# Token order, output stores and PSUM buffers of a fused pooled-attention and expert-routing kernel

## The chip, the core and the metric

The kernel runs on one core of a Trainium2 chip. The core has five engines that work side by side, each in the order of its own instruction list: TensorE for matmuls (PE; its weight loads are shown as PEld), VectorE (DVE), ScalarE (ACT), GpSimd (POOL) and SyncE (SP). They meet through semaphores. Sixteen DMA engines move data between HBM and SBUF; POOL and SP issue the transfers. Matmuls write to PSUM, which has 8 banks of 512 fp32 numbers in each of 128 partitions, and DVE and ACT read it out. The metric is device time in microseconds (us) of one execution.

## What is computed

```python
# q, k, v: (8, 8, 576, 64) float32: batch, head, token, dim
k_p = k.reshape(B, H, 72, 8, D).mean(axis=3)      # 576 tokens pooled to 72
v_p = v.reshape(B, H, 72, 8, D).mean(axis=3)
attn = softmax(q @ k_p^T / 8)                      # (B, H, 576, 72)
x = (attn @ v_p).transpose(0, 2, 1, 3).reshape(4608, 512)
# routing: normalised x against 8 normalised expert embeddings, / tau
expert_idx = argmax(logits, axis=1); gate_w = softmax(logits)[expert_idx]
for e in range(8):                                 # w1 (8,512,1024), w2 (8,1024,512)
    out[idx == e] = gate_w * (relu(x[idx == e] @ w1[e]) @ w2[e])
```

## The kernel before

The work goes in eight batches of 576 tokens. A batch has two halves: attention with routing, and the expert network (`ffn`). For each batch the kernel guesses one expert for all tokens from the mean of pooled v (steps GM, GC, GL, GD), and loads only that expert's weights. A loop at the end would add other experts' tokens; with these inputs it has no iterations.

**Loads.** POOL issues them in a fixed order: V0, K0, Q0, V1, and then for each batch b a group: PK (read the guessed expert number into a register), W1 of b, K of b+1, Q of b+1, W2 of b, V of b+2. They convert fp32 in HBM to fp16 in SBUF. So group b can't go before the guess of batch b, which needs V of b, which was the last load of group b-2. There are three buffers each for W1 and W2, two each for V, K and Q.

**Attention of one batch.** DVE adds V and K in groups of eight tokens (steps VA, VB, KA, KB, lines L301 to L315) and transposes q in 32x32 blocks (QT, L385). PE computes scores in four steps SC (two halves of 288 tokens, two groups of four heads, L415), each of which writes two double PSUM tiles. ACT takes the exponential (EX, L428), two per SC. For each of five chunks of 128 tokens (the fifth has 64 new ones), PE multiplies by pooled v (PV, L443) into a double tile, DVE normalises (XM, L451 and L453), PE transposes the result back (XT, L461), DVE copies it to SBUF (XE, L466) and ACT squares it for the norms (SQ, L472). PE's RT (L490, L495) gives the routing logits, and the steps RE, NA, NB, NC, ND make the gate `gm_all`.

**Token order.** Token s = 18*p + t of a batch (p of 32, t of 18) stands at column 32*t + p after QT, and all later steps keep that order. A chunk of 128 columns is therefore four values of t times 32 values of p: its 128 rows of `out` lie 18 rows apart in four interleaved sets.

**The expert network of one batch.** Eight steps H on PE (L548: 8 matmuls of 288 columns each, both halves into one double tile), each followed by a ReLU over 576 columns on ACT or DVE (HE, L557 or L559). Four steps Y (L563, 8 matmuls of 512 columns), two of them sharing one double tile, each followed by scaling with the gate (YE, L575 or L577) and a store of 128x512 fp32 by SP (ST, L622). The last 64 tokens go as YL (L569), which puts the two halves of the 512 output columns on partitions 0 to 63 and 64 to 127. DVE scales the first half (YF, L577), ACT the second (YG, L575), and SP stores both (SL, L644). The tokens' gates lie on partitions 64 to 127, so SP copies them to partitions 0 to 63 with a DMA of 64 x 4 bytes (NE, L539, `gl_all`); YF waits for it.

**PSUM.** One ring of four double tiles `pa` of 2 banks each serves every step.

**What sets the order.** `Plan.order` places every step by planned busy times (the numbers in `add`), priorities and free buffers, and the instructions of each engine are then written out in that order. On the chip each engine runs its list strictly in that order.

Of the kernel before, what the change touches and what calls it, by code (L numbers as in the profile page):

```python
# [142 lines left out]
def kernel(  # L143
# [36 lines left out]
    psum = Ring(lambda i: ps.tile([128, 1024], FP32, name=f"pa{i}"), 4)  # L180
# [91 lines left out]
    def attention(b, base):  # L272
# [52 lines left out]
        if b == 0:  # L325
            pv_, pk_ = Buf(psum), Buf(psum)
# [11 lines left out]
        else:  # L338
            add(n("VA"), 'DVE', 1.14, pr(-0.5), lambda: halve(vr.tile, 4), [n("V")], uses=[vr],
                late=0.1)  # L340
            add(n("VB"), 'DVE', 0.95, pr(-0.5), v_fold, [n("VA")], takes=[vp], uses=[vr],
# [3 lines left out]
            add(n("KB"), 'DVE', 1.0, pr(-0.2), k_fold, [n("KA")], takes=[kp], uses=[kr],  # L345
# [3 lines left out]
        pg = Buf(psum)  # L349
# [27 lines left out]
        add(n("GD"), 'DVE', 0.35, pr(-0.5), choose, [n("GL")], uses=[pg], late=0.1)  # L377
        add(n("GE"), 'DVE', 0.2, pr(0.5), onehot, [n("GD")], late=0.1)
# [12 lines left out]
        pk = Buf(psum)  # L391
# [10 lines left out]
        add(n("KE"), 'DVE', 0.25, pr(0.0), lambda: nc.vector.tensor_copy(  # L402
# [5 lines left out]
        for half in range(2):  # L408
            for a in range(NQ):
                pair = [Buf(psum), Buf(psum)]  # L410

                def score(a=a, half=half, pair=pair):
                    for c in range(2):
                        for m in range(QG):
                            nc.tensor.matmul(  # L415
                                out=pair[m // 2].tile[0:G, m % 2 * 512:m % 2 * 512 + HALF],
                                lhsT=kpT.tile[ts(m, R), a, c, :],
                                rhs=qT.tile[ts(m, R), a, ts(half, T // 2), c, :],
                                start=(c == 0), stop=(c == 1))

                f = 0.02 + 0.2 * half + 0.1 * a
                add(n("SC", half, a), 'PE', 0.35, pr(f), score,
                    [n("KE"), n("QT", a, half)], takes=pair, uses=[qT, kpT], late=0.22,
                    mode='r32')
                for i in range(2):
# [3 lines left out]
                            out=t.tile[:, :, ts(half, HALF)],  # L429
                            in_=p.tile[0:G].rearrange("g (r c) -> g r c", r=2)[:, :, 0:HALF],  # L430
# [5 lines left out]
        for c in range(NC):  # L436
            px, r, x, pt = Buf(psum), Buf(r_r), Buf(x_r), Buf(psum)
# [49 lines left out]
        pl = Buf(psum)  # L487
# [36 lines left out]
        def gate():  # L524
# [5 lines left out]
            nc.vector.tensor_reduce(out=gm_all[:, b], in_=lg, axis=AX.X, op=ALU.add)  # L530
            nc.vector.tensor_tensor(out=gm_all[:, b], in0=gm_all[:, b], in1=gate_all[:, b],
# [280 lines left out]
```

## Time and profile before

| what | value |
|---|---|
| median of 3 runs (lowest to highest) | 284.74 us (284.48 to 286.25) |
| the profiled execution | 285.62 us |
| its span, first to last instruction | 284.0 us |
| mean granted clock of PE | 0.879 |
| busy: PE, DVE, ACT, POOL | 205.8, 144.5, 119.4, 43.9 us |
| HBM read, written | 61.88 MB, 9.44 MB |

The span is the time that the engines' records cover. A row such as "x512 | 80.2, 313 | 33.4" gives a count, the busy time in us, the mean duration of one in ns, and the engine's idle time ahead of them. "[6.17 <-DVE y L577]" means that the engine stood idle for 6.17 us until that instruction released it. PE's clock has two levels here, 1.0 (2.4 GHz) and 0.5 (1.2 GHz). A "DMA share" is the mean busy share of the 16 DMA engines; two queues may be in one engine at the same time, so it can pass 1.

### The profile page before, as it was taken

The page shows a single profiled execution, that of the slowest core. Times are in us where ns is not written, and L with a number is a line of the kernel's source. Part 1 is how long each engine was busy: PE and PEld are TensorE (multiplying, and loading weights), DVE is VectorE, ACT ScalarE, POOL GpSimd, SP SyncE. Part 2 cuts the span into 40 slices and gives each one's busy share as a digit, 9 for nine tenths or more (in the row PEclk, how much of TensorE's full clock was granted, in tenths as well). Part 3 has the DMA queues.
Part 4 walks back from the last instruction along what each step waited for, and adds up shares of the span by engine and source line. Part 5 has one row for each costly group of instructions (what it writes and reads, how often), then busy time and mean ns, then how long its engine had stood idle before and what let it go on. Part 6 is the DMA issues. An engine that isn't in the chain of part 4 may idle for free.

```text
span 284.0 us, 5224 instructions
## 1 busy us (share of the span) xinstructions
PE 205.8 (72%) x2006; PEld 128.9 (45%) x2007; DVE 144.5 (51%) x398; ACT 119.4 (42%) x239; POOL 43.9 (15%) x59
## 2 busy tenths in 40 slices
PE   2898798868995597938995698904997069899600
PEld 1566664544563353624563354602555036476300
DVE  2178677945791557724792458514495043550200
ACT  2046285374457153453447254620542056454400
POOL 7052400700160005100060004100021000010000
PEclk9999999997999599896999599975899658999955
DMA  5979999999999937995299937992149421121120
GB/s 70 196 122 202 206 208 208 222 227 227 194 184 230 180 76 140 222 216 115 67 173 221 187 79 139 212 203 81 60 82 217 96 88 48 38 82 51 47 103 21
DMA packets 29147, 40.76 MB, mean 144 GB/s; under 512 B 4536, under 2 KB 14776, under 8 KB 29120
## 3 DMA queue, kind: packets, MB, share of 16 engines
q0 software_dynamic: 23184, 30.95, 62.5%
q1 hardware_dynamic: 5936, 9.46, 10.0%
q8 instruction: 16, 0.26, 0.4%
q14 instruction: 11, 0.09, 0.1%
HBM read 61.88 MB, written 9.44 MB: 251 GB/s over the span
## 4 chain that ended last, share of the span: by engine, by line
DMA 64%; PE 21%; DVE 4%; issue 3%; POOL 1%; ACT 1%; POOLq 1%; DVEq 0%
DMA vr<-in_v_dram 27%; DMA kr<-in_k_dram 19%; DMA gl_all<-gm_all 18%; PE pa L548 11%; PE pa L563 6%; PE pa L415 2%; DVE y L577 2%; PE pa L569 1%; POOL w L256 1%; DVE vr L301 1%; PE pa L322 1%; DVE xt_all L466 0%; ACT hT L557 0%; DVE kr L301 0%; POOLq L267 0%
## 5 line engine op out<-in xcount | busy, mean ns | idle before, releaser
L548 PE MATMUL pa<-xt_all,w 128*128 128x288 f16 x512 | 80.2, 313 | 33.4 <-DVE y L577 31.2
L548 PEld LDWEIGHTS <-w 128*128 128x128 f16 x512 | 51.3, 105 | 56.8 <-issue 41.6
L563 PE MATMUL pa<-w,hT 128*128 128x512 f16 x256 | 60.8, 383 | 4.9 <-DVE y L577 2.4
L428 ACT ACTIVATE at<-pa 72x576 f16<-72x576 f32 x64 | 37.4, 641 | 35.2 <-PE pa L415 35.1
L557 ACT ACTIVATE hT<-pa 128x576 f16<-128x576 f32 x49 | 31.8, 650 | 37.0 <-PE pa L548 35.0
L563 PEld LDWEIGHTS <-hT 128*128 128x128 f16 x256 | 24.6, 98 | 30.9 <-issue 7.3
L575 ACT ACTIVATE y<-pa,gm_all 128x512 f32<-128x512 f32 (+1 forms) x32 | 20.0, 630 | 39.9 <-PE pa L563 25.5
L472 ACT ACTIVATE sq<-x 128x512 f16<-128x512 f16 x40 | 25.1, 628 | 22.8 <-DVE x L453 18.8
L256 POOL DMA_DIRECT2D w<-in_moe_w_dram x8 | 6.4, 804 | 152.9 <-PE pa L563 120.2
L301 DVE TENSOR_TENSOR vr<-vr 72x2048 f16<-72x2048 f16 (+1 forms) x14 | 13.4, 954 | 32.8 <-DMA vr<-in_v_dram 32.6
L453 DVE TENSOR_TENSOR x<-pa,r 128x512 f16<-128x512 f32 x40 | 27.7, 691 | 1.7
L415 PE MATMUL pa<-qT,kpT 32*72 32x288 f16 x256 | 16.5, 341 | 11.4 <-DVE ssq_all L520 11.2
L385 DVE STREAM_TRANSPOSE qT<-qq 128x576 f16<-128x576 f16 x32 | 23.3, 756 | 1.5 <-DMA qq<-in_q_dram 1.5
L559 DVE TENSOR_SCALAR hT<-pa 128x576 f16<-128x576 f32 x15 | 11.4, 757 | 24.7 <-PE pa L548 24.4
L516 POOL TENSOR_TENSOR ssq_all<-ssq_all,half_c 128x5 f32<-128x5 f32 x8 | 9.9, 1242 | 51.1 <-ACT sq L472 51.1
L577 DVE TENSOR_SCALAR y<-pa,gl_all 64x256 f32<-64x256 f32 x8 | 3.8, 473 | 27.4 <-DMA gl_all<-gm_all 14.3
L466 DVE COPY xt_all<-pa 128x512 f16<-128x512 f16 (+1 forms) x40 | 14.8, 383 | 2.5 <-PE pa L461 2.4
L461 PE MATMUL pa<-ident_h,x 128*128 128x128 f16 x160 | 14.4, 224 | 2.2 <-DVE x L453 2.0
L301 DVE TENSOR_TENSOR kr<-kr 72x2048 f16<-72x2048 f16 (+1 forms) x14 | 13.3, 947 | 5.2 <-DMA kr<-in_k_dram 5.1
L415 PEld LDWEIGHTS <-kpT 32*72 32x72 f16 x256 | 5.5, 118 | 21.0 <-DVE kpT L402 11.6
L461 PEld LDWEIGHTS <-x 128*128 128x128 f16 x160 | 11.0, 100 | 8.8 <-DVE x L453 3.6
L443 PE MATMUL pa<-vpx,at 72*128 72x65 f16 x320 | 14.5, 194 | 0.0
(87 smaller groups left out, 174.6 us busy)
## 6 DMA issues: line engine op xcount, KB each, us to landing
w<-in_moe_w_dram POOLq DMA_DIRECT2D x16, 1024.0 KB, 24.2
out_dram<-y SPq DMA_DIRECT2D x32, 256.0 KB
vr<-in_v_dram POOLq DMA_DIRECT2D x8, 576.0 KB, 35.3
kr<-in_k_dram POOLq DMA_DIRECT2D x8, 576.0 KB, 25.7
qq<-in_q_dram POOLq DMA_DIRECT2D x7, 576.0 KB, 32.0
out_dram<-y SPq DMA_DIRECT2D x16, 64.0 KB
qq<-in_q_dram POOLq DMA_DIRECT2D x2, 288.0 KB, 10.1
gl_all<-gm_all SPq DMA_DIRECT2D x8, 0.2 KB
```

The source lines that it names most:

```text
L301: nc.vector.tensor_tensor(out=t[:, :, 0:m], in0=t[:, :, 0:m], in1=t[:, :, m:2 * m], op=ALU.add)
L385: nc.vector.transpose(out=qT.tile[:, a].rearrange("p t c e -> p (t c e)")[:, cols], in_=qq.tile[:, a, cols]),
L415: nc.tensor.matmul(out=pair[m // 2].tile[0:G, m % 2 * 512:m % 2 * 512 + HALF], lhsT=kpT.tile[ts(m, R), a, c, :], rhs=qT.tile[ts(m, R), a, ...
L428: lambda t=t, p=pair[i], half=half: nc.scalar.activation(out=t.tile[:, :, ts(half, HALF)], in_=p.tile[0:G].rearrange("g (r c) -> g r c", r ...
L453: nc.vector.tensor_tensor(out=x.tile, in0=pxv[:, :, 1:129].rearrange("p a (r d) -> p a r d", d=D), in1=r.tile.rearrange("p (a r) -> p a r" ...
L461: nc.tensor.transpose(out=pt.tile.bitcast(FP16)[:, ts(w, 128)], in_=xf[:, ts(w, 128)], identity=ident_h)
L466: nc.vector.tensor_copy(out=xt_all[:, b, :, c * 128:c * 128 + 128 - o], in_=pt.tile.bitcast(FP16)[:, 0:512].rearrange("p (w t) -> p w t", ...
L472: nc.scalar.activation(out=sq, in_=x.tile.rearrange("p a r d -> p (a r d)"), func=AF.Square, accum_out=ssq_all[:, b, c:c + 1])
L548: nc.tensor.matmul(out=p[:, half * 512:half * 512 + HALF], lhsT=w1v[:, kk, w // 2, w % 2, :], rhs=xt[:, kk, ts(half, HALF)], start=(kk == ...
L557: nc.scalar.activation(out=dst, in_=src, func=AF.Relu)
L563: nc.tensor.matmul(out=p, lhsT=hT[w][:, ts(c, 128)], rhs=w2[:, w // 2, w % 2, :], start=(w == 0), stop=(w == 7))
L575: nc.scalar.activation(out=dst, in_=src, func=AF.Copy, scale=g)
```

## The change

There are four parts. First, natural token order: SC reads 16 of the 32 values of p for all 18 t, and the exponential, which reads PSUM in steps of 18 and writes without gaps, puts token s at column s; each SC now needs both QT pieces of its heads. Second, a chunk is 128 rows of `out` that follow each other, so that a store's DRAM side is 128 x 512 and no longer 4 x 32 x 512, and the last one is 64 x 256 and no longer 2 x 32 x 256. Third, the eight gate copies by DMA (NE) are replaced by a multiply on DVE inside ND that writes partitions 0 to 63 from partitions 64 to 127. Fourth, PSUM becomes two double tiles `pa` (for SC and PV) and four single banks `pb` (for all the rest); H goes in halves of 288 columns, a bank and a ReLU for each half, and every Y has a bank of its own. Planned busy times are changed with it.

```diff
-    psum = Ring(lambda i: ps.tile([128, 1024], FP32, name=f"pa{i}"), 4)
+    psum = Ring(lambda i: ps.tile([128, 1024], FP32, name=f"pa{i}"), 2)
+    bank = Ring(lambda i: ps.tile([128, 512], FP32, name=f"pb{i}"), 4)
...
-                                rhs=qT.tile[ts(m, R), a, ts(half, T // 2), c, :],
+                                rhs=qT.tile[ts(m, R), a, :, c, ts(half, R // 2)],
...
-                add(n("SC", half, a), 'PE', 0.35, pr(f), score,
-                    [n("KE"), n("QT", a, half)], takes=pair, uses=[qT, kpT], late=0.22,
+                add(n("SC", half, a), 'PE', 0.27, pr(f), score,
+                    [n("KE"), n("QT", a, 0), n("QT", a, 1)], takes=pair, uses=[qT, kpT], late=0.22,
...
-                            out=t.tile[:, :, ts(half, HALF)],
-                            in_=p.tile[0:G].rearrange("g (r c) -> g r c", r=2)[:, :, 0:HALF],
+                            out=t.tile[:, :, ts(half, HALF)].rearrange(
+                                "g r (p t) -> g r p t", t=T),
+                            in_=p.tile[0:G].rearrange("g (r c) -> g r c", r=2)[:, :, 0:HALF]
+                            .rearrange("g r (t p) -> g r p t", t=T),
...
-            px, r, x, pt = Buf(psum), Buf(r_r), Buf(x_r), Buf(psum)
+            px, r, x, pt = Buf(psum), Buf(r_r), Buf(x_r), Buf(bank)
...
+            nc.vector.tensor_tensor(out=gl_all[:, b:b + 1], in0=gm_all[64:128, b, 4:5],
+                                    in1=gate_all[64:128, b, 4:5], op=ALU.mult)
...
-        add(n("NE"), 'SP', 0.1, pr(1.35), lambda: nc.sync.dma_start(
-            out=gl_all[0:64, b:b + 1], in_=gm_all[64:128, b, 4:5]), [n("ND")], mode=0.1, late=1.0)
...
+    def h_mm(xt, w1, w, half, p):
         w1v = w1.rearrange("p k (w c r) -> p k w r c", r=2, c=128)
...
+        for kk in range(4):
+            nc.tensor.matmul(out=p[:, 0:HALF], lhsT=w1v[:, kk, w // 2, w % 2, :],
+                             rhs=xt[:, kk, ts(half, HALF)], start=(kk == 0), stop=(kk == 3))
...
     def chunk_rows(o_b, c):
-        return o_b.rearrange("(p t) d -> t p d", t=T)[4 * c:4 * c + 4]
+        return o_b[ts(c, 128)]
...
     def last_rows(o_b):
-        return o_b.rearrange("(p t) (r d) -> r t p d", t=T, r=2)[:, 16:18]
+        return o_b[S - 64:S].rearrange("p (r d) -> r p d", r=2)
...
-    HE_ON, HE_BUSY = ('ACT', 'DVE'), (0.57, 0.67)
+    HE_ON, HE_BUSY = ('ACT', 'DVE'), (0.34, 0.38)
```

The order of instructions changes at three places that matter below. The first is SP's list at its first batch of stores; a row names the line, the destination and source buffers and the shape of the destination in DRAM. Before:

```order
L539 DMA gl_all_121<-gm_all_120 64x1
L622 DMA out_0_dram<-y0_109 4x32x512
L622 DMA out_0_dram<-y1_110 4x32x512
L622 DMA out_0_dram<-y2_111 4x32x512
L622 DMA out_0_dram<-y3_112 4x32x512
L644 DMA out_0_dram<-y4_113 2x32x256 x2
```

After:

```order
L624 DMA out_0_dram<-y0_111 128x512
L624 DMA out_0_dram<-y1_112 128x512
L624 DMA out_0_dram<-y2_113 128x512
L624 DMA out_0_dram<-y3_114 128x512
L646 DMA out_0_dram<-y4_115 64x256 x2
```

The gate copy is gone, and the slowest dimension of a store goes from 4 or 2 to 128 or 64.

The second place is DVE's list around the pooled sum of V of batch 4 (`vr0`, steps VA and VB) and YF of batch 1 (the row with `gl_all`). Before:

```order
L521 TENSOR_TENSOR lg_all_124<-lg_all_124,ssq_all_126 128x40
L369 CAST mx_all_129<-ix_all_128 128x1
L370 TENSOR_SCALAR eb_all_123<-irow_140,mx_all_129 128x8
L301 TENSOR_TENSOR vr0_73<-vr0_73 72x8x256
L301 TENSOR_TENSOR vr0_73<-vr0_73 72x8x128
L315 TENSOR_TENSOR vpx0_83<-vr0_73 72x4x128
L577 TENSOR_SCALAR y3_112<-pa0_61,gl_all_121 64x256
L525 TENSOR_REDUCE lmax_all_125<-lg_all_124 128x5
```

After:

```order
L576 TENSOR_SCALAR y3_114<-pb1_64,gl_all_123 64x256
L386 STREAM_TRANSPOSE qT1_80<-qq1_78 128x576
L506 TENSOR_REDUCE lmax_all_127<-pb3_66 128x5
L507 TENSOR_TENSOR oh_all_124<-pb3_66,lmax_all_127 128x40
L508 TENSOR_TENSOR lg_all_126<-pb3_66,lmax_all_127 128x40
L386 STREAM_TRANSPOSE qT1_80<-qq1_78 128x576 x2
L403 COPY kpT1_84<-pb2_65 128x288
L522 TENSOR_SCALAR ssq_all_128<-ssq_all_128 128x5
L523 RECIPROCAL ssq_all_128<-ssq_all_128 128x5
L524 TENSOR_TENSOR lg_all_126<-lg_all_126,ssq_all_128 128x40
L302 TENSOR_TENSOR vr0_75<-vr0_75 72x8x256
L528 TENSOR_REDUCE lmax_all_127<-lg_all_126 128x5
```

YF moved from behind the sums of V, which wait for a load, to a place well ahead of them.

The third place is ACT's list in the second part of an attention batch (`at` rows are exponentials, `hT` rows are ReLUs). Before, in batch 5:

```order
L557 ACTIVATE hT7_104<-pa1_62 128x576
L428 ACTIVATE at6_91<-pa2_63 72x2x288
L428 ACTIVATE at0_85<-pa3_64 72x2x288
L557 ACTIVATE hT0_97<-pa0_61 128x576
L428 ACTIVATE at4_89<-pa1_62 72x2x288
L428 ACTIVATE at5_90<-pa2_63 72x2x288
```

After, in batch 3:

```order
L556 ACTIVATE hT0_99<-pb2_65 128x288
L556 ACTIVATE hT1_100<-pb1_64 128x288
L556 ACTIVATE hT1_100<-pb3_66 128x288
L429 ACTIVATE at6_93<-pa1_62 72x2x288
L429 ACTIVATE at0_87<-pa0_61 72x2x288
L556 ACTIVATE hT3_102<-pb1_64 128x288
L429 ACTIVATE at4_91<-pa1_62 72x2x288
L429 ACTIVATE at5_92<-pa0_61 72x2x288
```

The exponentials, which took turns over four double tiles shared with the ReLUs, now take turns over two, so a pair of exponentials empties both tiles that the next SC needs; the ReLUs are twice as many, half as wide, and read `pb`.

## Rows read from the trace of the kernel before

**Rows 1.** The page: DMA queues (packets, MB, share of 16 engines' span)

```profile
q0 software_dynamic: 23184, 30.95, 62.5%
q1 hardware_dynamic: 5936, 9.46, 10.0%
```

**Rows 2.** The page: the chain that ended last, shares of the span

```profile
DMA vr<-in_v_dram 27%; DMA kr<-in_k_dram 19%; DMA gl_all<-gm_all 18%; PE pa L548 11%; PE pa L563 6%; PE pa L415 2%; DVE y L577 2%; PE pa L569 1%; POOL w L256 1%; DVE vr L301 1%; PE pa L322 1%; DVE xt_all L466 0%; ACT hT L557 0%; DVE kr L301 0%; POOLq L267 0%
```

**Rows 3.** Stretches of the span: busy time by engine, clock, DMA share, GB/s

```profile
core 0: us, PE busy (x) PEld busy (x) DVE busy (x) ACT busy (x) POOL busy (x), PEclk, DMA share, GB/s
20.00:40.00 20.00, 17.16 (x222) 12.23 (x219) 16.45 (x47) 11.03 (x24) 6.83 (x8) 1.00 1.17 204
100.00:108.00 8.00, 7.52 (x78) 4.86 (x75) 4.26 (x12) 3.96 (x9) 0.32 (x1) 1.00 0.30 71
246.00:256.00 10.00, 9.73 (x112) 7.04 (x110) 5.22 (x19) 5.28 (x11) 1.16 (x1) 1.00 0.27 84
```

**Rows 4.** Timeline of DVE: start, us, instruction, [idle before <-releaser]

```profile
63.49 1.22 DVE L301 TENSOR_TENSOR vr<-vr 72x2048 f16<-72x2048 f16 x1 [4.08 <-DMA vr<-in_v_dram]
...
92.50 1.94 DVE L301 TENSOR_TENSOR vr<-vr 72x2048 f16<-72x2048 f16 x2 [6.28 <-DMA vr<-in_v_dram]
...
190.33 1.94 DVE L301 TENSOR_TENSOR vr<-vr 72x2048 f16<-72x2048 f16 x2 [8.65 <-DMA vr<-in_v_dram]
...
228.76 0.48 DVE L577 TENSOR_SCALAR y<-pa,gl_all 64x256 f32<-64x256 f32 x1 [11.91 <-DMA gl_all<-gm_all]
```

**Rows 5.** Timeline of POOL: the issue of W1 of batch 4

```profile
107.68 0.82 POOL L256 DMA_DIRECT2D w<-in_moe_w_dram  x1 [23.28 <-PE pa L563]
```

**Rows 6.** Timeline of PE

```profile
65.15 2.08 PE L548 MATMUL pa<-xt_all,w 128*128 128x288 f16 x8 [2.73 <-DVE y L577]
...
88.74 0.44 PE L415 MATMUL pa<-qT,kpT 32*72 32x288 f16 x8
95.35 2.08 PE L548 MATMUL pa<-xt_all,w 128*128 128x288 f16 x8 [6.17 <-DVE y L577]
...
251.46 8.00 PE L548 MATMUL pa<-xt_all,w 128*128 128x288 f16 x64
259.30 7.07 PE L563 MATMUL pa<-w,hT 128*128 128x512 f16 x32
```

**Rows 7.** Groups of PE instructions from 190.3 us to the end

```profile
L548 PE MATMUL pa<-xt_all,w 128*128 128x288 f16 x160 | 25.3, 320 | 11.1 <-DVE y L577 11.1
L563 PE MATMUL pa<-w,hT 128*128 128x512 f16 x96 | 22.2, 379 | 1.4 <-DVE y L577 1.0 <-ACT y L575 0.3
L415 PE MATMUL pa<-qT,kpT 32*72 32x288 f16 x48 | 3.9, 420 | 11.2 <-DVE ssq_all L520 11.2
L443 PE MATMUL pa<-vpx,at 72*128 72x65 f16 x80 | 3.5, 194 | 0.0
L461 PE MATMUL pa<-ident_h,x 128*128 128x128 f16 x40 | 3.3, 219 | 0.0
L569 PE MATMUL pa<-w,hT 128*64 128x256 f16 x48 | 3.2, 276 | 0.0
```

**Rows 8.** Groups by shape on ACT and DVE, whole span

```profile
L428 ACT ACTIVATE at<-pa 72x576 f16<-72x576 f32 x64 | 37.4, 641 | 35.2 <-PE pa L415 35.1
L557 ACT ACTIVATE hT<-pa 128x576 f16<-128x576 f32 x49 | 31.8, 650 | 37.0 <-PE pa L548 35.0 <-DVE mx_all L369 1.4 <-DVE lg_all L521 0.5
L559 DVE TENSOR_SCALAR hT<-pa 128x576 f16<-128x576 f32 x15 | 11.4, 757 | 24.7 <-PE pa L548 24.4 <-ACT at L428 0.3
L531 DVE TENSOR_TENSOR gm_all<-gm_all,gate_all 128x5 f32<-128x5 f32 x8 | 1.3, 165 | 0.3
L329 ACT CAST kp<-pa 72x256 f16<-72x256 f32 x2 | 0.6, 368 | 12.0 <-PE pa L322 12.0
```

**Rows 9.** SP: its last stores in the timeline, and a wait of its queue

```profile
268.39 3.69 SPq L644 DMA_DIRECT2D out_dram<-y  x2
...
SPq L727 <- SPq L727: 5.7, 1, 5.7
```

More of the change, by code (lines that the diff above doesn't have):

```diff
@@ L340, in attention @@
                 late=0.1)
-            add(n("VB"), 'DVE', 0.95, pr(-0.5), v_fold, [n("VA")], takes=[vp], uses=[vr],
+            add(n("VB"), 'DVE', 1.0, pr(-0.5), v_fold, [n("VA")], takes=[vp], uses=[vr],
                 late=0.1)
@@ L344, in attention @@
                 late=0.1)
-            add(n("KB"), 'DVE', 1.0, pr(-0.2), k_fold, [n("KA")], takes=[kp], uses=[kr],
+            add(n("KB"), 'DVE', 1.08, pr(-0.2), k_fold, [n("KA")], takes=[kp], uses=[kr],
                 late=0.1)
-        pg = Buf(psum)
+        pg = Buf(bank)
         mv = Buf(mv_r)
@@ L376, in attention @@
         add(n("GL"), 'PE', 0.13, pr(-0.5), guess, [n("GC")], uses=[pg, mv], late=0.22)
-        add(n("GD"), 'DVE', 0.35, pr(-0.5), choose, [n("GL")], uses=[pg], late=0.1)
-        add(n("GE"), 'DVE', 0.2, pr(0.5), onehot, [n("GD")], late=0.1)
+        add(n("GD"), 'DVE', 0.42, pr(-0.5), choose, [n("GL")], uses=[pg], late=0.1)
+        add(n("GE"), 'DVE', 0.4, pr(0.5), onehot, [n("GD")], late=0.1)
         for a in range(NQ):
@@ L623, in ffn @@
                 out=chunk_rows(o_b, c), in_=y.tile), [n("YE", c)], uses=[y], mode=0.8, late=0.9)
-        p, y = Buf(psum), Buf(y_r)
+        p, y = Buf(bank), Buf(y_r)
         f = base + P * 16 / 17.0
         add(n("YL"), 'PE', 0.97, f, lambda: yl_mm([h.tile for h in hT], w2.tile, p.tile),
-            [n("W2")] + [n("HE", w) for w in range(8)], takes=[p], uses=[w2] + hT, late=0.22,
+            [n("W2")] + hs, takes=[p], uses=[w2] + hT, late=0.22,
             mode='c64')
@@ L631, in last @@
             rows = ts(r, 64)
-            scale_rows(y.tile[rows, 0:DH], p.tile[rows, r * 512:r * 512 + DH],
+            scale_rows(y.tile[rows, 0:DH], p.tile[rows, ts(r, DH)],
                        g[rows, 4:5] if r else gl_all[:, b:b + 1], 'ACT' if r else 'DVE')
-        add(n("YF"), 'DVE', 0.35, f - 2.0, lambda: last(0), [n("YL"), n("NE")], takes=[y],
+        add(n("YF"), 'DVE', 0.35, f - 2.0, lambda: last(0), [n("YL"), n("ND")], takes=[y],
             uses=[p], late=0.12)
@@ L701 @@
                 if s.fill:
-                    keep_warm((s.takes + s.uses)[0].tile if s.takes else
-                              [u for u in s.uses if u.ring is psum][0].tile, s.fill)
+                    keep_warm([u.tile for u in s.takes + s.uses if u.ring in (psum, bank)][0],
+                              s.fill)
                 s.run()
-        p = psum.tiles[0]
+        p = bank.tiles[0]
         nc.tensor.matmul(out=p[0:128, 0:B * NC * E], lhsT=ones_m[:, 0:128],
@@ L748 @@
             for w in range(8):
[L749 to L750 removed]
+                for j in range(2):
+                    p = bank.tiles[(2 * w + j) % 4]
+                    h_mm(xt_c, w1, w, j, p)
+                    h_relu(p, hT[w], j, 'ACT' if j else 'DVE')
             gl = gl_all[:, B:B + 1]
[L752 removed]
+            nc.vector.tensor_copy(out=gl, in_=gmx[64:128, 4:5])
             y, o = y_r.tiles[0], y_r.tiles[1]
             for c in range(5):
[L755 removed]
+                p = bank.tiles[c % 4]
                 if c < 4:
[L757 to L758 removed]
+                    y_mm(hT, w2, c, p)
+                    scale_rows(y, p, gmx[:, c:c + 1], 'DVE')
                     dst, cols = chunk_rows(o_b, c), DM
```

75 lines of the change are left out of this document (32 added, 43 removed).

## The prediction

> **What bounds the kernel now.** I began with the chain that ended last: 64% of the span is DMA, in the loads of V and K and in the gate copy [rows 2]. So the question is what makes loads late. The two queues' packets fill only 62.5 and 10.0% of 16 engines' time [rows 1], which looks like room. The table of stretches shows that it is not. While loads run alone, 20 to 40 us, the DMA share is full and 204 GB/s are moved. While stores run alone, 246 to 256 us, the share stands at 0.27, which is 4.3 of 16 engines, at 84 GB/s; and from 100 to 108 us, in the middle of the run, it is 0.30 at 71 GB/s [rows 3]. A load is done only when its slowest engine is done, and some four engines carry all stores on top of their share of the loads.
>
> A sum supports it. The loads are 30.95 MB, 3.87 MB a batch, and at 204 GB/s that takes 19.0 us. The stores use 10.0% of 16 engines over 284 us, 28.4 us of all, or 3.6 us a batch spread evenly, but 14.2 us on four engines. 19.0 + 14.2 = 33.2 us a batch. The timeline of DVE has V landing at 63.49 us (batch 3) and at 190.33 (batch 7), four periods of 31.7 us [rows 4]. That is close, so I take stores on four engines as the bound.
>
> Behind it the in-order lists pass the delay on. DVE waits for V with YF behind it, YF holds a PSUM tile, and PE waits 6.17 us for YF [rows 4, 6]. The gate copy shares the four engines; YF of batch 5 waited 11.91 us for it [rows 4].
>
> **The change part by part.**
>
> *Stores.* The bytes stay. What moves is how many engines carry them; no row shows a store of 128 x 512. Bounds: it stays on four engines and a period costs 33.2 us, or it runs on all 16 as the loads do [rows 3], and the period costs DMA 19.0 + 3.6 = 22.6 us. I take the second, since the only difference in shape between these stores and the weight loads goes away, and keep the first as a rival.
>
> The Trainium skill ("DMA: Bandwidth & Descriptors", section "Why a DMA increments its semaphore by 16 and not by 1") says that a transfer uses the largest number up to 16 that divides the slowest dimension of both sides. By that rule the stores used 4 and 2 engines and will use 16, and the period is 22.6 us; the trace's 4.3 engines agree for the shape of before, and nothing here shows the other.
>
> *The next bound.* With loads on time PE sets the pace. Its work for one batch ran without a long stall from 65.15 to 89.2 us [rows 6], 24.0 us. The first 8 H matmuls of it took 2.08 us at the lower clock, where 64 at the full clock took 8.00, so 1.00 for 8: 22.9 us at the full clock. DMA's 22.6 and PE's 22.9 are nearly equal, and lists in order can't catch up what either loses, so I add 0.8 us by choice: 23.7 us a period. The guess of an expert also has time: V of batch 4 arrived at 92.50 us and its weights were issued at 107.68 [rows 4, 5], 15.2 us, less than the 22.6 us that the group ahead keeps the DMA engines busy.
>
> *Gate copy.* Eight DMAs go, eight small multiplies come, at the 165 ns of their neighbour [rows 8]: 1.3 us over the span, on DVE, which has slack (144.5 us busy). Below, nothing; above, 1.3 us. I count nothing, since it is in ND, one batch ahead of YF. SP's list loses the item that waited for ND ahead of the next stores.
>
> *H in halves.* PE's matmuls are the same 512. The ReLUs double. ACT took 650 ns for 576 columns and 368 for a 256-column cast [rows 8], so about 0.4 us for 288, between 0.33 (half) and 0.65. DVE took 757 for 576; I take 0.46, between 0.38 and 0.76. The 64 become 128: with the same split of two thirds on ACT that adds about 6 us on each of ACT and DVE, 0.8 us a period on engines that were 42 and 51% busy. In a period of 23.7 us they are hidden by H itself: a half H takes 0.5 us of PE, and ACT and DVE together empty one each 0.22. If ACT is blocked by exponentials, the four banks hold 2 us of H.
>
> *Two double tiles.* Each SC now needs both, so it waits until both exponentials of the SC before have run: 2 x 0.641 [rows 8] and two hand-overs, some 1.6 us. The order puts two to four half H between (1.0 to 2.0 us of PE). I count no stall, and its price in a rival. Y in banks of their own saves the wait for the shared tile; PE's waits for YE are 1.4 us over the last three batches [rows 7], so I count nothing.
>
> *Strided exponential and SC.* ACT reads PSUM in steps of 18 of a 16-wide block, PE reads runs of 16 instead of 32. Bounds: nothing (the cast of rows 8 reorders runs of 32 at the rate of plain ones) or twice 0.641 us. I take nothing.
>
> *The end.* The last Y ends at 266.4 us, YL a microsecond later, and the span at 284.0 [rows 6]: 16.6 us. In these SP needs 3.69 us to issue the last two stores and then waits 5.7 us for them to land [rows 9]. With 16 engines the wait goes and the issue drops to about 1.1 (my estimate): 8.3 us are left.
>
> **The sum**, against the profiled span of 284.0 us. V of batch 3 lands at 62 us (63.49 before, with few stores so far); four periods of 23.7 bring V of batch 7 at 156.8; 1.7 us later PE starts on it, as at 65.15. What PE then had to do [rows 7] at the full clock is 160 x 0.125 + 96 x 0.221 = 41.2 us of H and Y, and 3.9 + 3.5 + 3.3 + 3.2 us, with small groups 56 us. That is 214.5, and with the end 222.8. The profiled execution took 285.62 us, 1.6 more than its span, and the median is 0.9 below it: **223.5 us**, range of this case 213 to 234.
>
> **The rivals.**
>
> *PSUM or the lists stall PE* (0.20). If a pair of exponentials with a ReLU or two ahead takes 2.0 to 2.4 us where the order gives 1.5, each SC stalls 0.5 to 0.9 us, 2 to 3.6 us a batch over some six batches: 235 to 245 us. For it: DVE and ACT must follow PE closely at 23 us. Against it: PE ran from 65 to 89 us in the old order with hardly a gap.
>
> *The strided exponential is slow* (0.08). At twice its time a pair costs 1.3 us more, with 28 SC after the first batch up to 36 us, part of it hidden: 245 to 262 us. The Trainium skill ("PSUM — Partial Sum Buffer", Specifications) says that access that isn't contiguous in 8-byte lines slows matmuls significantly; if that held for ACT's reads too, this rival would be the case. No run here shows it.
>
> *The stores don't spread* (0.06). Periods stay at 31.7, and only YF's waits for the gate go: 284.7 less 14 us, 262 to 275 us.
>
> *Less than the sum* (0.11). PE gets ahead early, the 0.8 us is not needed and short groups overlap: 203 to 213 us.
>
> *Slower than before* (0.03). The same place as the second rival, exponentials on PE's path: 62 us over 64 of them is 1.0 us each with none of it hidden, so it decides from 1.6 us per exponential on.
>
> **How the numbers follow.** The forecast has 0.50, and 0.02 goes to no measurable difference. The range of 207 to 247 leaves out half of the fast rival, most of the second, all of the third and the last, 0.19 in all. About 1% is what a measurement of this kernel can tell from no change; faster than that has 0.95, within it 0.02, slower 0.03.
>
> **What would show it.** Right: DMA share near 1 through all loads, never 0.25 to 0.3 while a load is out; V landing every 22 to 25 us; PE's clock at 1.0 from 65 us to the end; no wait on `gl_all`; SP's last wait under 2 us. Wrong: a share of 0.27 in the last 20 us (stores not spread); exponentials over 0.75 us; PE waiting for EX ahead of SC, or ACT busy over 70% in a period.

## The result and the profile after

The changed kernel takes 219.76 us in the median (219.18 to 223.29, four runs) against 285.5 us for the kernel before beside it: a ratio of 0.769, 95% interval 0.764 to 0.774. The prediction was 223.5 us. The profiled execution that came with the result took 223.29 us, 3.5 above the median, and V of each batch from batch 2 on landed 3.2 to 4.3 us late in it; the same kernel, profiled once more beside the experiments, took 219.74 us (span 217.9), and the rows below are of that second profile.

First the two DMA queues and the chain that ended last, to be read against [rows 1, 2] (packets, MB, share of 16 engines' span; then shares of the span).

```profile
q0 software_dynamic: 23184, 30.95, 81.5%
q1 hardware_dynamic: 5904, 9.46, 13.1%
...
DMA vr<-in_v_dram 36%; PE pb L550 15%; PE pb L562 11%; DVE x L456 3%; PE pa L416 3%; ACT at L429 2%; DVE vr L302 2%; DVE qT L386 2%; DVE kr L302 2%; PE pb L568 1%; PE pa L446 1%; DVE xt_all L469 1%; DVE r L454 1%; PE pb L464 1%; ACT hT L556 1%
```

The shares rose, the work didn't. 81.5% of 217.9 us is 177.6 us of 16 engines, and 62.5% of 284.0 us was 177.5; for the stores it is 28.5 us and was 28.4. Taken together the packets take as long as before. The stores' packets only lie on more engines at a time. K's loads and the gate copy are gone from the chain; V's are left.

The table of stretches, with the lines that answer to [rows 3]: loads early, the middle of the run, and one microsecond in which only a 256 KB store is under way.

```profile
core 0: us, PE busy (x) PEld busy (x) DVE busy (x) ACT busy (x) POOL busy (x), PEclk, DMA share, GB/s
...
100.00:108.00 8.00, 6.84 (x86) 4.64 (x85) 7.76 (x21) 4.24 (x11) 1.37 (x2) 1.00 1.13 245
20.00:40.00 20.00, 17.82 (x222) 13.00 (x222) 15.56 (x46) 13.11 (x32) 5.83 (x7) 1.00 1.17 204
...
209.00:210.00 1.00, 1.00 (x18) 0.80 (x16) 0.00 (x0) 0.69 (x1) 0.00 (x0) 1.00 0.69 262
```

The middle of the run has a DMA share of 1.13 where it had 0.30, and 245 GB/s where it had 71. The lone store runs at a share of 0.69 and 262 GB/s; stores alone had 0.27 and 84.

VectorE's timeline, with its first sum of V for batches 3, 4 and 7 and the gated multiply of the last rows of batch 5 just ahead of the third, as in [rows 4]. Behind it stand GpSimd's issue of V of batch 7 with its time to landing, and two pieces of the chain that ended last (start, us, what): V of batch 6, which is the last load in that chain, and VectorE's sum of it.

```profile
61.61 1.22 DVE L302 TENSOR_TENSOR vr<-vr 72x2048 f16<-72x2048 f16 x1
...
86.33 1.22 DVE L302 TENSOR_TENSOR vr<-vr 72x2048 f16<-72x2048 f16 x1 [2.43 <-DMA vr<-in_v_dram]
...
153.03 0.47 DVE L576 TENSOR_SCALAR y<-pb,gl_all 64x256 f32<-64x256 f32 x1
153.73 1.21 DVE L302 TENSOR_TENSOR vr<-vr 72x2048 f16<-72x2048 f16 x1
...
L246 POOL DMA_DIRECT2D vr<-in_v_dram x1: 862/862/862, 123.3 to 123.3; - x1
DMA to landing us min/median/max: 25.2/25.2/25.2
...
99.33 30.42 DMA vr<-in_v_dram
129.77 1.22 DVE vr L302
```

From batch 3 to batch 7 it is (153.73 - 61.61) / 4 = 23.0 us a period from sum to sum, where it was 31.7. The multiply that waited 11.91 us for its gate waits for nothing.

In the kernel before, these sums waited for their loads. Here that holds, within 1.1 us, up to batch 6, whose V lands at 129.75 us and is summed at once; from batch 3 to there a period is 22.7 us. V of batch 7 lands at 123.3 + 25.2 = 148.5 us and lies for 5.2 us until VectorE comes to it, and behind V of batch 6 no engine waits for a load any more. So below, "the last V" is the start of VectorE's sum of V of batch 7, and landings are named where they differ.

The last products on PE, SP's last stores and the longest wait of its queue after them, and PE's two largest groups from the last V to the end, against [rows 6, 7, 9].

```profile
202.17 7.07 PE L562 MATMUL pb<-w,hT 128*128 128x512 f16 x32
209.17 1.06 PE L568 MATMUL pb<-w,hT 128*64 128x256 f16 x16
...
210.84 1.11 SPq L646 DMA_DIRECT2D out_dram<-y  x2
...
SPq L811 <- DVEq L811: 1.6, 1, 1.6
...
L550 PE MATMUL pb<-xt_all,w 128*128 128x288 f16 x177 | 23.7, 286 | 0.0
L562 PE MATMUL pb<-w,hT 128*128 128x512 f16 x96 | 22.2, 379 | 0.0
```

The last product ends at 210.2 us and the span at 217.9: 7.7 us, where it was 16.6. In the stretch from the last V to the end, PE's products wait for nothing (0.0 us of idle ahead of both groups; it was 11.1 and 1.4).

The whole fall of the span, 284.0 - 217.9 = 66.1 us, falls into four stretches: V of batch 3 comes 1.9 us earlier (63.5 to 61.6); four periods shrink from 126.8 to 92.1 us, 34.7; from the last V to the last product it is 56.5 us where it was 77.0, 20.5; the end gives 9.0 (16.6 to 7.7, rounded).

### The profile page after: what moved, and what is told of

Its sections match the earlier page's. It is cut to its first block, busy times and chain, and to the rows that moved or that the text cites. A ratio compares the mean times of both kernels' runs of the same rounds, so it can differ in the third digit from the quotient of the medians.

```text
span 221.4 us, 5250 instructions
## 1 busy us (share of the span) xinstructions
PE 196.6 (89%) x2009; PEld 124.9 (56%) x2010; DVE 147.8 (67%) x427; ACT 124.3 (56%) x282; POOL 43.4 (20%) x59
## 4 chain that ended last, share of the span: by engine, by line
PE 43%; DMA 29%; DVE 14%; issue 5%; ACT 4%; POOL 2%; POOLq 1%; DVEq 0%; ACTq 0%
DMA vr<-in_v_dram 29%; PE pb L550 15%; PE pb L562 11%; PE pb L653 3%; PE pb L323 3%; PE pa L416 3%; DVE x L456 3%; PE pa L653 3%; ACT at L429 2%; DVE qT L386 2%; DVE kr L302 2%; PE pb L568 1%; PE pa L446 1%; DVE xt_all L469 1%; DVE vr L302 1%
## 5 line engine op out<-in xcount | busy, mean ns | idle before, releaser
L550 PE MATMUL pb<-xt_all,w 128*128 128x288 f16 x512 | 71.3, 286 | 5.2 <-ACT y L574 1.5
L562 PE MATMUL pb<-w,hT 128*128 128x512 f16 x256 | 59.8, 379 | 0.6 <-ACT y L574 0.6
L550 PEld LDWEIGHTS <-w 128*128 128x128 f16 x512 | 47.3, 98 | 22.9 <-issue 12.5
L556 ACT ACTIVATE hT<-pb 128x288 f16<-128x288 f32 x91 | 36.5, 409 | 20.3 <-PE pb L550 17.7
L475 ACT ACTIVATE sq<-x 128x512 f16<-128x512 f16 x40 | 25.2, 629 | 31.8 <-DVE x L456 28.1
L574 ACT ACTIVATE y<-pb,gm_all 128x512 f32<-128x512 f32 (+1 forms) x33 | 20.8, 630 | 16.6 <-PE pb L562 12.1
L558 DVE TENSOR_SCALAR hT<-pb 128x288 f16<-128x288 f32 x37 | 16.7, 453 | 11.1 <-PE pb L550 10.7
L464 PE MATMUL pb<-ident_h,x 128*128 128x128 f16 x160 | 14.7, 220 | 3.0 <-DVE x L456 1.9
L469 DVE COPY xt_all<-pb 128x512 f16<-128x512 f16 (+1 forms) x40 | 14.8, 383 | 2.9 <-PE pb L464 2.9
L446 PEld LDWEIGHTS <-at 72*128 72x128 f16 x320 | 13.4, 98 | 1.7 <-issue 0.3
L653 PEld LDWEIGHTS <-ones_m 128*128 128x128 f16 x92 | 10.5, 120 | 5.5 <-issue 2.9
```

Of the source, the lines that this page charges most:

```text
L446: nc.tensor.matmul(out=px.tile[:, o:o + 65], lhsT=at[h // 2].tile[:, h % 2, c0:c0 + 128], rhs=vp.tile[:, h // 2, 1 + h % 2 * 65:66 + h % 2 ...
L464: nc.tensor.transpose(out=pt.tile.bitcast(FP16)[:, ts(w, 128)], in_=xf[:, ts(w, 128)], identity=ident_h)
L475: nc.scalar.activation(out=sq, in_=x.tile.rearrange("p a r d -> p (a r d)"), func=AF.Square, accum_out=ssq_all[:, b, c:c + 1])
L550: nc.tensor.matmul(out=p[:, 0:HALF], lhsT=w1v[:, kk, w // 2, w % 2, :], rhs=xt[:, kk, ts(half, HALF)], start=(kk == 0), stop=(kk == 3))
L556: nc.scalar.activation(out=dst, in_=src, func=AF.Relu)
L562: nc.tensor.matmul(out=p, lhsT=hT[w][:, ts(c, 128)], rhs=w2[:, w // 2, w % 2, :], start=(w == 0), stop=(w == 7))
```

## The experiments

### Which part of the change does it: the stores' shape

Store shapes of before in the changed kernel:

```diff
-        return o_b[ts(c, 128)]
+        return o_b.rearrange("(p t) d -> t p d", t=T)[4 * c:4 * c + 4]
...
-        return o_b[S - 64:S].rearrange("p (r d) -> r p d", r=2)
+        return o_b.rearrange("(p t) (r d) -> r t p d", t=T, r=2)[:, 16:18]
```

> The changed kernel with the store shapes of before (4x32x512 and 2x32x256, written with the views that the kernel before used) and everything else as changed; as the tokens now stand in natural order, the output's rows land in another order. Theory (a store whose slowest dimension is 4 is carried by about 4 of the 16 queue engines, and the loads behind it wait for those): the period of a batch goes back to 19.0 us of loads plus 14.2 us of stores, about 31 to 33 us, V of the last batch lands some 8 us a batch later than in the changed kernel, and the time is 265 to 285 us, near before. Rival (the halves of PSUM, the single banks and the gate made the gain): the period stays near 23 us and the time is 218 to 226 us.

Measured: 274.69 us (273.9 to 275.47), ratio to before 0.960, interval 0.949 to 0.971. Two lines of VectorE (V of batches 3 and 7), the stretch in which PE does its last products and only stores are under way, and SP's last two stores with the wait behind them:

```profile
66.52 1.22 DVE L302 TENSOR_TENSOR vr<-vr 72x2048 f16<-72x2048 f16 x1 [5.03 <-DMA vr<-in_v_dram]
...
194.37 1.22 DVE L302 TENSOR_TENSOR vr<-vr 72x2048 f16<-72x2048 f16 x1 [5.14 <-DMA vr<-in_v_dram]
...
250.00:256.00 6.00, 6.00 (x30) 2.72 (x28) 0.00 (x0) 2.34 (x4) 0.00 (x0) 1.00 0.21 64
...
256.67 1.06 PE L568 MATMUL pb<-w,hT 128*64 128x256 f16 x16
...
258.33 3.23 SPq L646 DMA_DIRECT2D out_dram<-y  x2
...
SPq L729 <- SPq L729: 5.8, 1, 5.8
```

The period is back at 32.0 us. Against the changed kernel the span grows by 55.7 us, and it can be placed: 4.9 at the third V, 35.7 in the four periods, 6.9 from the last V to the last product (63.4 against 56.5 us), and 8.2 at the end (15.9 against 7.7), where issue and wait of SP stand as in [rows 9].

The other way round, the kernel before with the new store shapes alone (the two lines of the diff above, exchanged):

> The kernel before with the two new store shapes alone (128x512 and 64x256), nothing else changed; as its tokens stand in the old order, the output's rows land in another order. Theory (the stores' spread is the whole of the gain in the period): 220 to 235 us, with V landing every 23 to 25 us; what is left to the changed kernel is the gate by DMA at the end, up to 6 us. Rival (spread stores give nothing until PSUM and the lists are changed): 270 to 285 us. Between: 240 to 265 us would say that PE, with PSUM as four double banks and an order planned for longer operations, cannot follow the quicker loads.

Measured: 222.09 us (221.31 to 222.88), ratio 0.776, interval 0.766 to 0.786. So two lines of the diff give 63.9 of the some 66 us, without the PSUM layout, the lists that go with it or the gate on VectorE. The rival that PE could not follow quicker loads in the old layout is out.

Is it the shape, or where the bytes fall? Here each store writes the same contiguous 256 KB as in the changed kernel, in a shape whose slowest dimension is 4:

```diff
-        return o_b[ts(c, 128)]
+        return o_b[ts(c, 128)].rearrange("(p a) d -> a p d", a=4)
```

> The changed kernel with each store written as 4x32x512 (2x32x256 for the last rows) over the very same contiguous 128 (64) rows of the output, so that the bytes fall in the same 256 KB as in the changed kernel and only the shape has 4 as its slowest dimension; rows land in another order within a chunk. Theory (the slowest dimension counts, not where the bytes fall): about 4 engines again, 265 to 285 us. Rival (stores spread over rows far apart in memory are slow, contiguous ones quick): 218 to 226 us.

Measured: 274.08 us (274.07 to 274.09). The stretch below has stores alone on the queues, near the 0.27 of [rows 3]:

```profile
236.00:242.00 6.00, 4.63 (x63) 3.23 (x62) 3.75 (x12) 2.63 (x7) 1.16 (x1) 1.00 0.25 82
```

And the opposite: rows in groups far apart in the output, 16 groups (the first new line) and 8 (the second), the last rows likewise:

```diff
-        return o_b[ts(c, 128)]
+        return o_b.rearrange("(a r) d -> a r d", a=16)[:, c:32:4]
+        return o_b.rearrange("(a r) d -> a r d", a=8)[:, c:64:4]
```

> The changed kernel with its stores written as 16x8x512 (16x4x256 for the last rows): 16 groups of rows that lie far apart in the output, landing in another order. Theory (16 engines again, and where the rows fall makes no difference): 218 to 223 us, like the changed kernel. Rival (rows in one contiguous 256 KB are needed for the speed): 235 us or more.

> The changed kernel with its stores written as 8x16x512 (8x8x256 for the last rows), rows landing in another order. A dose between 4x32x512 (274 us) and 128x512 (220 us). Theory (a store is carried by as many engines as its slowest dimension counts): 8 engines, the stores of a batch take them 3.6 x 16 / 8 = 7.2 us, the period is 19.0 + 7.2 = 26.2 us instead of 23.1, V of the last batch lands four periods later by 3.1 us each, near 170 us, and the time is 228 to 236 us. Rival (any shape of three dimensions is as slow as 4x32): 265 to 280 us.

Measured: 219.57 us (219.44 to 219.70) with 16 groups, 234.41 us (233.53 to 235.30) with 8. V of batches 3 and 7 in the timeline of VectorE, first of the kernel with 16 groups:

```profile
62.12 1.22 DVE L302 TENSOR_TENSOR vr<-vr 72x2048 f16<-72x2048 f16 x1 [0.15 <-DMA vr<-in_v_dram]
...
153.41 1.22 DVE L302 TENSOR_TENSOR vr<-vr 72x2048 f16<-72x2048 f16 x1
```

and of the one with 8, with a stretch at its end that has stores alone on the queues:

```profile
65.12 1.22 DVE L302 TENSOR_TENSOR vr<-vr 72x2048 f16<-72x2048 f16 x1 [2.44 <-DMA vr<-in_v_dram]
...
168.02 1.21 DVE L302 TENSOR_TENSOR vr<-vr 72x2048 f16<-72x2048 f16 x1
...
222.00:228.00 6.00, 2.77 (x25) 1.38 (x22) 1.90 (x8) 1.69 (x3) 0.00 (x0) 0.95 0.48 145
```

The periods are from batch 3 to batch 7, once from sum to sum and once from landing to landing of V:

| slowest dimension | period, sums | period, landings | 19.0 + 3.6 x 16 / n | time |
|---|---|---|---|---|
| 4 (rows apart) | 32.0 us | 32.0 us | 33.4 us | 274.7 us |
| 4 (same rows) | 31.8 us | 31.8 us | 33.4 us | 274.1 us |
| 8 | 25.7 us | 23.8 us | 26.2 us | 234.4 us |
| 16 | 22.8 us | 21.8 us | 22.6 us | 219.6 us |
| 128 (the changed kernel) | 23.0 us | 21.8 us | 22.6 us | 219.6 us |

The three doses come in the order of the sum, and the place of the rows in memory makes no difference. With 8, 16 and 128 VectorE takes the last V up 7.6, 4.2 and 5.2 us after it has landed, so the landings are the better measure of the queues; by them the sum is 0.8 to 2.4 us too large, most with 8. Adding loads and stores overstates the period a little. Stores alone ran at shares of 0.27 with 4 and 0.48 with 8, which is 4.3 and 7.7 of 16 engines. The rule of the Trainium skill that the prediction weighed ("DMA: Bandwidth & Descriptors", section "Why a DMA increments its semaphore by 16 and not by 1") is borne out at 4, 8 and 16, and 128 acts as 16 does.

### What sets the pace now: DMA or PE

The prediction had 22.6 us of DMA and 22.9 of PE in a period and named PE as the next bound. Half of each second product is left out here:

```diff
-        for w in range(8):
+        for w in range(4):
             nc.tensor.matmul(out=p, lhsT=hT[w][:, ts(c, 128)], rhs=w2[:, w // 2, w % 2, :],
-                             start=(w == 0), stop=(w == 7))
+                             start=(w == 0), stop=(w == 3))
```

> The changed kernel with only half of each second product (4 of its 8 matmuls for each chunk of 128 rows) left in, so PE has about 3.5 us less to do per batch: tells what sets the changed kernel's period of 23.1 us. If the loads set it (by my sum 22.6 us of DMA a batch against 22.9 of PE): V of the last batch lands within 4 us of 157.3 us, and the time falls only by the end's saving, by 4 to 10 us, to 210 to 216 us. If PE sets it: V7 lands 3 us a batch earlier, about 10 to 14 us in all, and the time falls by 20 us or more, to 195 to 200 us.

Measured: 216.64 us (215.25 to 218.03), some 3 us below the changed kernel. The sum of V of batch 7, the stretch of the four periods, the stretch from 130 to 172 us and PE's longest wait in it, here:

```profile
154.29 1.22 DVE L302 TENSOR_TENSOR vr<-vr 72x2048 f16<-72x2048 f16 x1
...
65.00:154.00 89.00, 74.30 (x844) 47.46 (x840) 72.35 (x204) 53.84 (x123) 19.85 (x23) 0.94 1.15 225
...
130.00:172.00 42.00, 34.68 (x387) 21.96 (x387) 35.75 (x96) 24.62 (x57) 5.88 (x7) 0.97 1.09 212
...
PE pb L464 <- DVE x L456: 5.6, 7, 1.7
```

and the two stretches in the changed kernel:

```profile
65.00:154.00 89.00, 81.08 (x901) 50.89 (x900) 71.34 (x201) 53.61 (x122) 19.88 (x23) 1.00 1.15 224
...
130.00:172.00 42.00, 39.73 (x425) 25.00 (x423) 36.08 (x97) 25.23 (x58) 5.90 (x7) 1.00 1.08 212
```

PE has 6.8 us less to do in these 89 us, and the loads neither come earlier (V of batch 6 lands at 130.3 us against 129.75) nor move more (225 against 224 GB/s). Up to V of batch 6 the loads set the pace. Behind it no engine of the changed kernel waits for a load: PE is busy for 39.7 of the 42 us and VectorE for 36.1. With half of Y, PE has 5 us less to do there and the last V still comes no earlier (154.29 against 153.73, where the expectation's 157.3 is the same sum in the execution of 223.29 us). Now PE waits 5.6 us for VectorE's x, so VectorE's list is close behind PE's. The saving that there is comes later: 59.0 us from the last V to the end of the span against 64.2. It came out slightly smaller than I had expected (210 to 216 us); PE's waits for VectorE and its lower clock are in it, and no run separates them.

### The rest of the change: PSUM, gate and token order

The changed kernel and three others were timed side by side.

> The changed kernel itself, as the measure for the three runs beside it: 218 to 222 us.

Measured: 219.58 us (218.32 to 220.18), ratio to before 0.7688 (0.7651 to 0.7725).

Without the PSUM part (four double tiles, H and its ReLU over 576 columns, the planned times of before):

```diff
-    psum = Ring(lambda i: ps.tile([128, 1024], FP32, name=f"pa{i}"), 2)
-    bank = Ring(lambda i: ps.tile([128, 512], FP32, name=f"pb{i}"), 4)
+    psum = Ring(lambda i: ps.tile([128, 1024], FP32, name=f"pa{i}"), 4)
...
-    def h_mm(xt, w1, w, half, p):
+    def h_mm(xt, w1, w, p):
...
-            p, y = Buf(bank), Buf(y_r)
+            if c % 2 == 0:
+                p = Buf(psum)
+            i, y = c % 2, Buf(y_r)
```

> The changed kernel without its PSUM part: four double banks, first products of 576 columns, the planner's durations of before; natural order, new stores and the gate on VectorE stay. With the new stores alone the time was 222.1 us, 2.3 us above the changed kernel; this and the next two runs share that rest out. Theory (the loads set the period with either layout, and the halves only cost ACT and DVE 6 us each beside it): 218 to 222 us, within 1% of the changed kernel, perhaps 1 us below it. Rival (single banks let PE run on where it waited 4.6 us for DVE's y in the run with the new stores alone): 222 to 226 us.

Measured: 221.85 us (221.18 to 222.56), ratio 0.7777 (0.7743 to 0.7811). The intervals stand apart: my theory of no effect falls, and the part is worth 2.3 us. The trace says where. The last V comes at 154.17 us against 153.73 in the changed kernel, so the periods are equal within 0.2 us. From there to the end these are all of PE's waits (us in total, times, longest):

```profile
PE pa L565 <- DVE y L579: 1.0, 2, 0.6
PE pa L550 <- DVE y L579: 0.7, 2, 0.4
PE pa L550 <- ACT hT L559: 0.4, 1, 0.4
PE pa L710 <- ACT y L577: 0.4, 1, 0.4
PE pa L565 <- ACT y L577: 0.3, 1, 0.3
```

and in the changed kernel from its last V on:

```profile
PE pb L493 <- DVE xt_all L469: 0.2, 1, 0.2
```

2.8 us of waits against 0.2, and from the last V to the last product 58.9 us against 56.5. The wait of 0.4 us at L710 stands behind the last product; of the other 2.4 us, 2.0 are for a y to leave its tile, which two Y share. In the periods such waits cost little, since the loads set the pace up to batch 6; behind the last V PE of the changed kernel is never idle, and each of them counts. With the old store shapes the PSUM part made no difference that these runs show: the kernel with it takes 274.69 us, the one further down that has neither it nor the new token order 274.76.

The gate copied by DMA again:

```diff
-            nc.vector.tensor_tensor(out=gl_all[:, b:b + 1], in0=gm_all[64:128, b, 4:5],
-                                    in1=gate_all[64:128, b, 4:5], op=ALU.mult)
...
+        add(n("NE"), 'SP', 0.1, pr(1.35), lambda: nc.sync.dma_start(
+            out=gl_all[0:64, b:b + 1], in_=gm_all[64:128, b, 4:5]), [n("ND")], mode=0.1, late=1.0)
```

> The changed kernel with the gate of the last rows copied by a DMA on SP's queue again, as before. Theory (the 11.91 us wait of before was a copy queued behind slow stores, so it goes with them): 219 to 222 us, at most 2 us above the changed kernel, and the VectorE instruction that reads the gate waits under 2 us. Rival (the copy itself is slow because the loads fill the queues): YF waits 5 us or more in several batches and the time is 224 us or more.

Measured: 221.07 us (219.78 to 223.54), ratio 0.7762 (0.7714 to 0.7811). The interval overlaps that of the changed kernel, and of the six runs two took 223.3 and 223.5 us while the other four lie between 219.8 and 221.3, so 1.5 us is not settled. The trace, of the fastest of them, shows no price: span 217.8 us against 217.9, the last V at 153.6, and in VectorE's waits no entry for the copy, where before had two of 14.3 us together.

The gate on VectorE in the kernel before, stores and PSUM as they were:

> The kernel before with the gate of the last rows computed on VectorE instead of copied by a DMA, its slow stores left as they are. Theory (the loads behind slow stores set the time; the copy's waits on VectorE lay beside them): 278 to 286 us, at most 3% below before. Rival (the copy's wait of 11.91 us held VectorE, and with it a batch): 260 to 272 us.

Measured: 274.76 us (273.58 to 275.94), ratio 0.959 (0.953 to 0.966). Neither range held it: I had taken the copy's wait as lying beside the loads' lateness. V of batch 7 and the gated multiply of batches 5 and 6:

```profile
193.71 1.22 DVE L301 TENSOR_TENSOR vr<-vr 72x2048 f16<-72x2048 f16 x1 [6.71 <-DMA vr<-in_v_dram]
...
218.74 0.48 DVE L577 TENSOR_SCALAR y<-pa,gl_all 64x256 f32<-64x256 f32 x1 [2.92 <-ACT y L575]
...
241.57 0.47 DVE L577 TENSOR_SCALAR y<-pa,gl_all 64x256 f32<-64x256 f32 x1 [1.12 <-DMA out_dram<-y]
```

The last V comes 3.4 us later than before, so the periods gained nothing. The gain lies wholly behind it: 63.2 us from the last V to the last product, where it was 77.0, and the 13.8 between them is about the two waits for the copy, 14.3 us, the longer of them in [rows 4]. Behind the last V, VectorE's pooled sum of K waits for its load in neither kernel, so no late load covered those waits. The copy cost 11 us behind slow stores and about nothing behind quick ones; the two gains don't add.

Token order of before in the changed kernel (scores read and the exponential writes one run of 288 columns):

```diff
-                                rhs=qT.tile[ts(m, R), a, :, c, ts(half, R // 2)],
+                                rhs=qT.tile[ts(m, R), a, ts(half, T // 2), c, :],
```

> The changed kernel with scores and exp reading and writing their columns in the order of before (one run of 288, not 16-wide strides), so the output's rows land in another order: the price of the natural order alone. Theory (the strided reads cost nothing: the exp took 641 ns before and after): 218 to 222 us, exp 641 ns. Rival (the strides cost PE or ACT something that the durations hide): more than 1% below the changed kernel.

Measured: 219.32 us (219.03 to 222.69), ratio 0.7689, as the changed kernel. Groups by shape, first of this kernel, then of the changed one with its two ReLU groups:

```profile
L429 ACT ACTIVATE at<-pa 72x576 f16<-72x576 f32 x64 | 38.2, 640 | 4.8 <-PE pa L416 4.7
```

```profile
L429 ACT ACTIVATE at<-pa 72x576 f16<-72x576 f32 x64 | 38.2, 640 | 4.8 <-PE pa L416 4.6
L556 ACT ACTIVATE hT<-pb 128x288 f16<-128x288 f32 x91 | 36.4, 408 | 21.0 <-PE pb L550 16.7 <-DVE lg_all L524 1.7
L558 DVE TENSOR_SCALAR hT<-pb 128x288 f16<-128x288 f32 x37 | 16.7, 452 | 11.1 <-PE pb L550 10.7
```

The exponential takes 640 ns in either order, and a score matmul 294 ns. The Trainium skill's line on access that isn't contiguous ("PSUM — Partial Sum Buffer", Specifications), on which one rival stood, is about matmuls; ACT's strided reads of PSUM follow no such rule here.

### A quicker version

If the loads set the pace up to V of batch 6, an idle stretch of the queues ahead of it is time lost. There is one. GpSimd waits for the first batch's choice before it issues that batch's weights, and nothing is queued behind. K of batch 1 can go ahead of it:

```diff
-    loads = ["V0", "K0", "Q0.0", "Q0.1", "V1"]
+    loads = ["V0", "K0", "Q0.0", "Q0.1", "V1", "K1"]
...
-            loads += [f"K{b + 1}", f"Q{b + 1}.0"]
+            loads += ([f"K{b + 1}"] if b else []) + [f"Q{b + 1}.0"]
```

> The changed kernel with K of batch 1 loaded ahead of the first expert's weights. In the changed kernel GpSimd waits 10.0 us from 6.8 us on for the first batch's choice before it may issue that load, and behind it nothing is queued: the DMA share falls to 0.45 between 16 and 18 us. Theory (the loads set the pace up to 157 us, so a hole in them is lost time): K1 fills the hole of some 2 us, V of the last batch lands 1 to 2.5 us earlier, and the time is 217 to 219 us against 219.6. Rival (the first weights now come 2.6 us later and PE's first products with them, so PE loses what DMA gains): 219 to 222 us.

Measured: 215.94 us (215.47 to 216.37, six runs), ratio to before 0.7539 (0.7510 to 0.7568), against 0.7688 (0.7651 to 0.7725): 1.7% below the changed kernel, intervals apart, and below both ranges of the expectation. The stretch of the hole, with the DMA share and GB/s in the last two columns, first the changed kernel:

```profile
16.00:18.00 2.00, 1.79 (x21) 1.21 (x19) 1.68 (x5) 0.08 (x1) 1.26 (x2) 1.00 0.45 75
```

then this one, with VectorE's sums of V of batches 2, 6 and 7:

```profile
16.00:18.00 2.00, 1.90 (x24) 1.42 (x22) 1.96 (x6) 0.00 (x0) 0.90 (x2) 1.00 1.28 199
...
39.81 1.22 DVE L302 TENSOR_TENSOR vr<-vr 72x2048 f16<-72x2048 f16 x1
...
126.44 1.22 DVE L302 TENSOR_TENSOR vr<-vr 72x2048 f16<-72x2048 f16 x1
...
150.10 1.22 DVE L302 TENSOR_TENSOR vr<-vr 72x2048 f16<-72x2048 f16 x1 [1.11 <-DMA vr<-in_v_dram]
```

The hole is filled, and V of batch 2 lands at 37.5 us instead of 41.0, though VectorE, busy with other steps, comes to it only 1.3 us earlier (39.81 against 41.07). V of batch 6, the last load that the changed kernel waits for, lands at 125.7 us instead of 129.75, and its sum comes 3.3 us earlier; the last V comes 3.6 us earlier, nearly the whole of the gain of 3.8 us in the span. V of batch 7 itself lands 1.6 us later here (150.1 us against 148.5), but in the changed kernel it lay for 5.2 us, and here VectorE waits for it. So the hole was time lost, as expected. The lead isn't steady in between (0.4 us at the landing of batch 3, 4.8 at that of batch 4), and the queues move 228 GB/s instead of 223 between 62 and 150 us; why they run fuller there after one load was moved, no run here tells.

## Why the prediction was right

*The bound.* Stores on about four engines, with loads that wait for the slowest engine: shown by four kernels that change only the shape. My sum overstated the old period (33.2 against 31.7 us) and came near the new one (22.6 against 22.7 from batch 3 to batch 6, the stretch in which the loads are waited for). With 8 groups it was 2.4 us above the landings.

*The sum, term by term*, against the span of 217.9 us: V of batch 3 at 62 us was 61.6; four periods of 23.7 us were of 23.0 from sum to sum, 2.7 us less in all; 1.7 + 56 us from there to the last product were 56.5; the end of 8.3 us was 7.7. Together 222.8 against 217.9, and over half of the difference is the 0.8 us a period that I had added by choice. One step held in its number and not in its path: the sum lets PE start on V of batch 7 1.7 us after it lands, but V landed at 148.5 us, 8.3 us ahead of my 156.8, and waited 5.2 us for VectorE. The last of the four periods, from V of batch 6 to the last V, is 24.0 us of PE's and VectorE's own pace. That this lies near the loads' 22.7 is luck.

*The next bound.* Here the step failed in part, although its number nearly held. I wrote that PE sets the pace once loads are on time, and added 0.8 us because lists in order lose what either engine loses. Up to V of batch 6 it is DMA, at 22.7 us a period: with half of Y left out V of batch 6 came no earlier. PE becomes the bound only behind it, where it is busy for 39.7 of 42 us from 130 to 172 us, with VectorE close behind (36.1), and without a gap from the last V on. VectorE stood in my sum as an engine with slack.

*The gate copy.* I counted nothing for its removal, and with the new stores that is what the traces show. That the 11.91 us wait was worth 11 us in the old kernel I had only in the price of a rival, that the stores don't spread and the gate's waits go (262 to 275 us): the kernel with the old shapes took 274.7.

*H in halves.* The estimates of 0.4 and 0.46 us were 408 and 452 ns. They added 4.6 us on ACT and 5.3 on DVE where I had 6 each, and held PE nowhere for long: the rival of stalls (235 to 245 us) did not come. I counted nothing for Y in banks of their own, from 1.4 us of waits in [rows 7]; the PSUM part as a whole was worth 2.3 us, and this is the one term here that I set too small.

*The strided exponential* cost nothing, as counted. The *slower* rival hung on it and falls with it.

*What I had said would show it* is there: share above 1 through the loads, VectorE's sums of V every 19.8 to 24.7 us (23.0 in the mean, single ones a little outside my 22 to 25; the landings lie 18.8 to 25.0 apart), PE's clock at 1.00 through 65 to 154 us, no wait on `gl_all`, and SP's longest wait at the end 1.6 us.

## What to carry to other kernels

Look at the DMA share in a stretch where only one kind of transfer runs: a share of a quarter can mean that its shape uses a quarter of the engines, as it did here, and that every load that shares them is late by it, though over the whole span the queues look as if a quarter of their time were left. Then make the slowest dimension of that access 16 or a multiple of it, before buffers and lists are retuned; it was two lines here, and the rest of the change is worth some 2 us behind them. A wait that is dear behind a bottleneck can cost nothing once the bottleneck is gone, so gains measured one at a time don't add. And ask of every load whether its consumer takes it up when it lands: the start of the consumer tells that only where it had been waiting.

## What the runs showed that I had not expected

Where the rows of a store lie in memory made no difference that these runs show: 16 groups far apart 219.57 us, one contiguous block 219.58. The same contiguous 256 KB written as 4 groups: 274.08.

In the kernel with half of Y, PE's granted clock mostly fell where PE had been left waiting. Its page, in 40 slices of 5.3 us, PE's busy tenths and the clock that was granted:

```profile
PE   0988889985899398997999858985999589989960
...
PEclk9999999999699979997999996999999999999997
```

Three of its four drops ahead of the end stand right behind a slice in which PE was busy for only 3 or 5 tenths (two more such slices have no drop behind them). Over 65 to 154 us the clock is 0.94 in the mean of its two levels, and 1.00 with all of Y. So part of the work left out was paid back in slower matmuls (a matmul of Y took 394 ns in the mean against 379), and an experiment that takes work from PE can show less than the work it takes.
